# Attention with a gated MLP on one core: reciprocals read in a row, softmax sums by DMA transpose in units 0 to 115, the last head group regrouped, denser MLP tiles in the second slot

## Chip, core and metric

One core of a Trainium2 chip runs the whole kernel. The metric is the device time of one execution in microseconds; the kernel before took 1253.55 us, the median of 3 runs (1253.39 to 1253.73). One further execution was profiled: 1253.59 us, of which 1251.8 us lie between its first and its last instruction (the span).

## Reference

All tensors are bfloat16. There are 2048 tokens of width 512, 32 heads of 128 and 2048 cached keys for each head.

```
xn = layernorm(x)                                   # 2048 x 512
# A: attention
q  = xn @ wq                                        # 32 heads of 128
p  = softmax(q @ k_cache^T * 128**-0.5)             # per head 2048 x 2048
s  = concat(p @ v_cache) @ wo                       # 2048 x 512
# B: gated MLP
h  = gelu(layernorm(xn) @ w1)
hs = shift_four_column_groups_by(1, -1, 2, -2)(h) @ w2
x1 = xn + hs
g  = silu(x1 + gelu(layernorm(x1) @ w3) @ w4)
out = x + s * g
```

## The kernel before

The MLP comes first. Its last product, for token tiles 8 to 15 (128 tokens each), is held back and mixed into the first attention units as filler for TensorE: 8 tiles of 14 matmuls each (`held_part`, with VectorE's addition and ScalarE's tanh for each in `held_out`).

The attention is 128 units, `units = [(g, qt, hh)]`: 8 groups `g` of 4 heads; in each group 4 query blocks `qt` of 512 tokens; in each block the 4 heads `hh`. A unit has 8 slots `p`, and a slot `n = 8*u + p` covers 256 keys. One Python loop over `n` writes out the order of work by hand, and every instruction is pinned to that order on its engine.

Within a unit:

- `s_slot`: two matmuls of 128x512 make scores in PSUM (two buffers of 2 banks, `ps_s`), and one ScalarE exp writes `pT`.
- `pv_run`: two matmuls multiply `pT` by V into `ps_o` (two buffers), `lag` slots later. The lag is 5 in units 0 to 7, grows to 10 by unit 12, and falls back to 5 from unit `PV1` (111) on.
- `q_mm`, `q_copy`: four matmuls make the next unit's query into the PSUM tile `xa`; VectorE copies it. Sixteen units have their query made ahead, in the MLP phase (`q_ahead`: units 0 to 8, 112 to 116, 126 and 127).
- `add_first`, `add_next`, `add_last`: VectorE adds the four `pT` tiles of a unit into `acc` and folds that to 128x512 (lines 297 to 308). The rest of the row sum runs over partitions, and it has two forms.
  - `sums` (units outside `TURN`): four matmuls of one column (`ps_sum`, line 325) with `acc` as weights, then a reciprocal (line 327).
  - `turn` and `turned_sums` (units in `TURN`, which is 12 to 107): a DMA transposes `acc` into `tT` (line 333), VectorE sums along the row (line 338) and takes the reciprocal.
- Both forms write the 512 reciprocals to DRAM (`dr`) and read them back on all partitions (`bcast`: `rb`, line 346), both on SyncE's DMA queue, which works in order.
- `norm` (line 358) multiplies `ps_o` by `rb` into `oT`. A plain sum leaves on partition p the reciprocals of the queries 4p to 4p+3, a turned one those of the queries p, p+128, p+256 and p+384. So in a turned unit `rb` lies in another order than `ps_o`, and `norm` reads `rb` (float32) with a step of four elements and everything else in a row.
- `wo_mm`, `wo_post`: when the 4 heads of a block are normed, each of its 4 token tiles takes 4 matmuls with `oT` as weights into the PSUM tile `xm`, and VectorE adds the result into `sacc`. In the last group it also applies the gate and the residual (lines 411, 420, 422; for the last two query blocks 404 and 392) and the tile is stored by SyncE's queue.

Plain units do two output matmuls a slot in slots 4 and 5, turned units one a slot in slots 3 to 6. Near the end, units 125 and 126 work on two token tiles each. A block written out by hand ends unit 127 (UB): the sums and `norm` of unit 126 (UA), then `late_sums`, `late_o`, `last_wo` and the last four tiles. There, the last `norm` (unit 126) waits for the last `rb`.

```
late = 0 if u <= NU - 5 * HG else 2 if u <= NU - 5 * HG + 2 else 1
if p == (7 if u - 2 in TURN else 2 + late) and 2 <= u:
    norm_queue(u - 2)
if p == 3 + late and 1 <= u and u - 1 not in TURN:
    sums(u - 1)
```

Of the kernel before, what the change touches and what calls it, by code (L numbers as in the profile page):

```python
# [10 lines left out]
FP32 = mybir.dt.float32  # L11
BF16 = mybir.dt.bfloat16
# [5 lines left out]
def kernel(  # L18
# [16 lines left out]
    P = nc.NUM_PARTITIONS  # L35
# [3 lines left out]
    Sq, D = x2d.shape  # L39
    _, H, Sk, Dh = A_k_cache.shape  # L40
# [52 lines left out]
    psX = ent(pool("psX", 1, PSUM))  # L93
# [14 lines left out]
    def mm(out, lhsT, rhs, start, stop):  # L108
        pin(nc.tensor.matmul(out=out, lhsT=lhsT, rhs=rhs, start=start, stop=stop))  # L109
# [11 lines left out]
    LATE = (QT - 2, QT - 1)  # L121
    GY = NG - 2
    NU = len(units)
    TURN = range(3 * HG, NU - 5 * HG)
    PV0, PV1 = 2 * HG, NU - 5 * HG + 3
    NS = NU * SPU
    kTs, vBs, wqs, wos, oTs, st = {}, {}, {}, {}, {}, {}
    todo = defaultdict(list)
# [171 lines left out]
    def add_next(u, i):  # L300
        a = st[u]["acc"]
        pin(nc.vector.tensor_tensor(out=a[:], in0=a[:], in1=st[u]["pT"][i][:], op=ALU.add))  # L302

    def add_last(u):
        add_next(u, 3)
        a = st[u]["acc"]
        pin(nc.vector.tensor_tensor(out=a[:, 0:2, :], in0=a[:, 0:2, :], in1=a[:, 2:4, :], op=ALU.add))  # L307
        pin(nc.vector.tensor_tensor(out=a[:, 0, :], in0=a[:, 0, :], in1=a[:, 1, :], op=ALU.add))  # L308
# [20 lines left out]
        pin(nc.sync.dma_start(out=s["dr"][:], in_=rc[:]))  # L329

    def turn(u):
        st[u]["tT"] = pS.tile([P, 4, P], BF16, tag="tT", bufs=2, name="tT")
        pin(nc.sync.dma_start_transpose(out=st[u]["tT"][:], in_=st[u]["acc"][:, 0, :]))

    def turned_sums(u):
# [13 lines left out]
    def norm(u):  # L349
        g, qt, hh = units[u]  # L350
        s = st.pop(u)
        if hh == 0:
            oTs[(g, qt)] = pB.tile([P, HG, 512], BF16, tag="oT", bufs=2, name="oT")
        o, rb, to = s["o"][:], s["rb"][:], oTs[(g, qt)][:, hh, :]
        if u in TURN:
            o, to = (x.rearrange("k (j p) -> k j p", j=4) for x in (o, to))
            rb = rb.rearrange("k (p j) -> k j p", j=4)
        pin(nc.vector.tensor_tensor(out=to, in0=o, in1=rb, op=ALU.mult))  # L358

    wo_box = {}  # L360
# [3 lines left out]
        wos[h] = pB.tile([P, D], BF16, tag="wo", bufs=2 * HG, name="wo_h")  # L364
        pin(nc.sync.dma_start(out=wos[h][:], in_=A_wo[h * Dh:(h + 1) * Dh, :]))

    def wo_mm(g, t, hhs):
        if hhs[0] == 0:
            wo_box[0] = psX.tile([P, D], FP32, tag="xm", name="ps_wo")
        oT = oTs[(g, t // 4)]  # L370
        ts = t % 4
        for hh in hhs:
            mm(wo_box[0][:], oT[:, hh, ts * P:(ts + 1) * P], wos[g * HG + hh][:], hh == 0, hh == HG - 1)

    fin = {}

# [73 lines left out]

    def last_wo(ts, ps, hhs=(0, 1, 2), stop=False):
        for hh in hhs:
            mm(ps, oTs[(NG - 1, QT - 1)][:, hh, ts * P:(ts + 1) * P], wos[(NG - 1) * HG + hh][:],
               hh == 0, stop and hh == HG - 2)

    def last_act(ps, scale):
# [27 lines left out]
    for jc in range(DC):  # L484
        b = BASE_J[jc]
# [37 lines left out]
    made = []  # L523

    def q_ahead(u):
        q_mm(u, range(DC), ("xa", "xm")[len(made) % 2])
        q_copy(u, nc.scalar)
        made.append(u)
# [27 lines left out]
        x1(t, ps)  # L556
    for t in range(4):
        stats(xall[:, t, :], mv2, rs2, t)
    for u in range(NU - 4 * HG, NU - 3 * HG):
        q_ahead(u)  # L560
    for t in range(4, 8):
        x1(t, m2(t))
# [2 lines left out]
    m1(1536, 512)  # L565
    for t in range(8, 11):
        x1(t, m2(t))
    for u in (2 * HG, NU - 12, NU - 2, NU - 1):
        q_ahead(u)
    for t in range(4, 8):  # L570
        stats(xall[:, t, :], mv2, rs2, t)
# [39 lines left out]
    pB = left.enter_context(pool("pB", reuse_waits="tile"))  # L611
# [3 lines left out]
    pS = None  # L615
    for h in range(HG):
        load_wo(h)
    for g in range(NG - 1):
        b = (g * QT + QT - 1) * HG
# [6 lines left out]
            at((b + (-3, -3, 0, 0)[hh]) * SPU + (5, 7)[hh % 2], lambda h=h: load_w(h))  # L626
            at((b - 4 - hh // 2) * SPU + (5, 7)[hh % 2], lambda h=h: load_wo(h))

    HELD = 7
    heldps = {}  # L630

    def held_part(t, a, b, tag="xm"):
        if a == 0:
            heldps[t] = psX.tile([P, 512], FP32, tag=tag, name="ps_m")
        m4(t, heldps[t], range(a, b))

    def held_out(t, n):
        x2(t, heldps.pop(t))
        th = {}
        at(n + 2, lambda: th.update(a=gate_tanh(t)))  # L640
        at(n + 4, lambda: gate_silu(t, th["a"]))

    def held_mm(n):
        u, p = divmod(n, SPU)
        if u == 0 and p < 2:
            held_part(8, 7 * p, 7 * p + 7, "xa")
            if p == 1:
                held_out(8, n)
        elif u == 0:
            held_part(9, FC * (p - 2) // 6, FC * (p - 1) // 6)  # L650
            if p == SPU - 1:
                held_out(9, n)
        elif u < HELD:
            if p < SPU - 1:
                held_part(9 + u, 2 * p, 2 * p + 2)
            if p == SPU - 2:
                held_out(9 + u, n)

    wo_todo = deque()
    pv_at = [0]  # L660

    def pv_run(n):
        u = n // SPU
        if u < PV0:
            lag = LAG
        elif u < PV0 + LAG:
            lag = LAG + u - PV0 + 1
        elif u < PV1:
            lag = 2 * LAG
        else:  # L670
            lag = max(LAG, 2 * LAG - (u - PV1 + 1))
        while pv_at[0] <= min(n - lag, NS - 1):
            pv_slot(*divmod(pv_at[0], SPU))
            pv_at[0] += 1

    def norm_queue(u):
        norm(u)
        gg, qq, hh = units[u]
        if hh == HG - 1:
            wo_todo.extend((gg, 4 * qq + ts) for ts in range(4))  # L680
            if gg == NG - 1 and qq not in LATE:
                fin_load(4 * qq)

    UA, UB = NU - 2, NU - 1

    def wo_slot(part, n, each=2):
        gg, t = wo_todo[0]
        if part < HG // each:
            wo_mm(gg, t, tuple(range(part * each, (part + 1) * each)))
            return  # L690
        wo_todo.popleft()
        wo_post(gg, t, n)
        if gg == NG - 1 and t % 4 < 3 and t + 1 not in fin and t // 4 not in LATE:
            fin_load(t + 1)

    q_plan = defaultdict(list)
    for v in range(1, NU):
        if v not in made:
            for dc in range(DC):
                k = dc - 1 if v - 2 in TURN else dc // 2  # L700
                q_plan[(v - 1) * SPU + k].append((v, (dc,)))

    for n in range(UB * SPU):
        u, p = divmod(n, SPU)
        extra = len(wo_todo) > 3 and u < 2 * HG + 2 and pS is not None or u >= UA - 1
        s_slot(u, p)
        pv_run(n)
        for v, dcs in q_plan.get(n, ()):
            q_mm(v, dcs)
        if p == 0 and u - 2 in TURN:  # L710
            turned_sums(u - 2)
        if p == 1 and u - 2 in TURN:
            bcast(u - 2)
        if p == 0 and 1 <= u:
            add_last(u - 1)
        if p == 3 and u - 1 in TURN:
            turn(u - 1)
        if p == 0:
            twice = extra
        if twice and p < 3:  # L720
            wo_slot(p, n)
        if p == (3 if u - 1 in TURN else 2) and u + 1 not in made:
            q_copy(u + 1)
        late = 0 if u <= NU - 5 * HG else 2 if u <= NU - 5 * HG + 2 else 1
        if p == (7 if u - 2 in TURN else 2 + late) and 2 <= u:
            norm_queue(u - 2)
        if p == 3 + late and 1 <= u and u - 1 not in TURN:
            sums(u - 1)
        if p == 4 + late and 1 <= u and u - 1 not in TURN:
            bcast(u - 1)  # L730
        each, p0 = (1, 3) if u - 2 in TURN else (2, 4)
        if p0 <= p <= p0 + HG // each and wo_todo and pS is not None:
            wo_slot(p - p0, n, each=each)
        if p == 4:
            add_first(u)
        if p == 6:
            add_next(u, 2)
        held_mm(n)
        for fn in todo.pop(n, ()):
            fn()  # L740
        if n == HELD * SPU - 1:
            right.close()
            pS = right.enter_context(pool("pS", side="right", reuse_waits="tile"))

# [2 lines left out]
    n = UB * SPU  # L747
    ident2 = pS.tile([P, P], BF16, tag="ident2", name="ident2")
    pin(nc.vector.tensor_scalar(out=ident2[:], in0=ident[:], scalar1=2.0, scalar2=None, op0=ALU.mult))
    for p in range(SPU):  # L750
        s_slot(UB, p)
        pv_run(n + p)
        if p == 0:
            add_last(UA)
        if p < 2:
            wo_slot(p, n + p)
        if p == 3:
            norm(UB - 2)
            sums(UA)
            wo_slot(2, n + p)  # L760
        if p == 4:
            bcast(UA)
            add_first(UB)
        if p == 6:
            add_next(UB, 2)
# [8 lines left out]
    ps = {0: bank(psX, "xm")}  # L774
# [81 lines left out]
```

## Time and profile before

| what | value |
|---|---|
| median of 3 runs | 1253.55 us (1253.39 to 1253.73) |
| profiled execution | 1253.59 us, span 1251.8 us |
| TensorE busy | 1237.9 us, 99% of the span |
| ScalarE busy | 1101.5 us, 88% |
| VectorE busy | 1031.9 us, 82% |
| attention units start | 123.0 us |
| unit 127 starts | 1230.6 us |
| DMA queue of SyncE | 100.33 MB in 223488 packets, 37.7% of 16 engines' time |

PE is TensorE's matmul, PEld its weight load, DVE VectorE, ACT ScalarE, SPq SyncE's DMA queue. A group line of the profile names the source line, the engine, the operation, the output and inputs by the program's names, their shapes and the count; after the bar come busy us, mean ns of one, and the idle time before the group's instructions with what ended it. All matmuls go through one helper, so they share line 109 and are told apart by their tiles. A stretch row gives start and end, length, busy time with the number of instructions, granted clock and DMA.

### The profile page before, as it was taken

To read this page: it belongs to the slowest core of one execution; us is meant where nothing else is said; L and a number is where in the kernel's file an instruction comes from. 1 tells how busy PE (TensorE), PEld (TensorE's weight loads), DVE (VectorE), ACT (ScalarE), POOL (GpSimd) and SP (SyncE) were. 2 spreads that over 40 slices of the span, in tenths; PEclk is the share of its full clock that TensorE was granted. 3 is DMA by queue.
4 is the path that set the end of the run, shared out by engine and by line. 5 is a ranking of instruction groups with operands and counts; after the bars stand their busy time and mean duration, and the time that the engine had idled before them with its cause. 6 is when DMAs were issued, how large, how long until landed. Compare 5 with 4: busy or idle time off the path is not lost.

```text
span 1251.8 us, 16270 instructions
## 1 busy us (share of the span) xinstructions
PE 1237.9 (99%) x5814; PEld 597.8 (48%) x5931; DVE 1031.9 (82%) x1430; ACT 1101.5 (88%) x1117; POOL 35.5 (3%) x91
## 2 busy tenths in 40 slices
PE   9999999999999999999999999999999999999998
PEld 4444444444444444444444444444444444444443
DVE  7621567788888988888888888888888999978888
ACT  5344888999999999999999999999999999998886
POOL 5310000000000000000000000000000000000000
PEclk9999999999999999999999999999999999999999
DMA  6482112444244523453244514353244424442222
GB/s 180 112 161 54 18 26 43 87 106 81 53 89 93 118 52 64 97 110 77 68 83 106 103 39 93 80 119 68 57 100 102 103 66 86 99 92 50 68 56 59
DMA packets 224945, 103.86 MB, mean 83 GB/s; under 512 B 176928, under 2 KB 208160, under 8 KB 224864
## 3 DMA queue, kind: packets, MB, share of 16 engines
q1 hardware_dynamic: 223488, 100.33, 37.7%
q0 software_dynamic: 672, 1.84, 0.8%
q8 instruction: 46, 0.75, 0.3%
q10 hardware_dynamic: 704, 0.66, 0.2%
q14 instruction: 35, 0.29, 0.1%
HBM read 67.90 MB, written 2.36 MB: 56 GB/s over the span
## 4 chain that ended last, share of the span: by engine, by line
PE 96%; DVE 2%; issue 1%; ACT 1%; DMA 1%; POOL 0%; SPq 0%; DVEq 0%; ACTq 0%
PE ps_s L109 39%; PE ps_o L109 36%; PE ps_q L109 9%; PE ps_wo L109 9%; PE ps_m L109 2%; DVE acc L302 0%; DMA rb<-dr 0%; PE ps_sum L109 0%; PE ps_w L109 0%; DMA xin<-in_A_x_dram 0%; ACT qT L277 0%; DVE y L392 0%; DVE xall L420 0%; ACT pT L291 0%; DVE sacc L411 0%
## 5 line engine op out<-in xcount | busy, mean ns | idle before, releaser
L291 ACT ACTIVATE pT<-ps_s 128x1024 bf16<-128x1024 f32 x1024 | 1035.2, 1024 | 75.4 <-PE ps_s L109 27.8
L109 PE MATMUL ps_s<-qT,kT 128*128 128x512 bf16 x2041 | 607.6, 379 | 0.6
L109 PE MATMUL ps_o<-pT,vb 128*128 128x512 bf16 x1962 | 588.9, 379 | 0.5
L302 DVE TENSOR_TENSOR acc<-acc,pT 128x2048 bf16<-128x2048 bf16 x255 | 309.3, 1213 | 83.7 <-ACT pT L291 80.2
L109 PEld LDWEIGHTS <-kT 128*128 128x128 bf16 x2048 | 230.3, 113 | 226.6 <-issue 0.8
L109 PEld LDWEIGHTS <-vb 128*128 128x128 bf16 x2048 | 200.3, 98 | 226.4 <-issue 0.4
L109 PE MATMUL ps_wo<-wo_h,oT 128*128 128x512 bf16 x492 | 177.8, 379 | 2.1
L109 PE MATMUL ps_q<-xnT,wq_h 128*128 128x512 bf16 x481 | 172.9, 379 | 2.1
L297 DVE TENSOR_TENSOR acc<-pT 128x2048 bf16<-128x2048 bf16 x128 | 155.9, 1218 | 6.1 <-ACT pT L291 5.9
L358 DVE TENSOR_TENSOR oT<-ps_o,rb 128x512 bf16<-128x512 f32 x127 | 124.6, 981 | 15.8 <-DMA rb<-dr 15.3
L307 DVE TENSOR_TENSOR acc<-acc 128x1024 bf16<-128x1024 bf16 x127 | 87.9, 692 | 4.3
L275 DVE CAST qT<-ps_q 128x512 bf16<-128x512 f32 x112 | 76.5, 683 | 0.3 <-PE ps_q L109 0.3
L109 PEld LDWEIGHTS <-oT 128*128 128x128 bf16 x508 | 48.5, 98 | 56.1 <-DVE oT L358 0.7
L109 PEld LDWEIGHTS <-wq_h 128*128 128x128 bf16 x484 | 47.2, 98 | 56.1 <-issue 0.2
L411 DVE TENSOR_TENSOR sacc<-ps_wo,sacc 128x512 f32<-128x512 f32 x96 | 66.3, 691 | 3.2 <-PE ps_wo L109 2.7
L338 DVE TENSOR_REDUCE sm<-tT 128x4 f32<-128x512 bf16 x96 | 65.5, 682 | 0.5 <-DMA tT<-acc 0.4
L308 DVE TENSOR_TENSOR acc<-acc 128x512 bf16<-128x512 bf16 x127 | 54.0, 425 | 4.3
L242 ACT ACTIVATE h2T<-ps_s 128x1024 bf16<-128x1024 f32 x28 | 28.7, 1025 | 24.0 <-PE ps_s L109 24.0
L109 PE MATMUL ps_s<-xn2T,w_sb 128*128 128x512 bf16 x219 | 48.6, 379 | 0.3
L109 PEld LDWEIGHTS <-w_sb 128*128 128x128 bf16 x336 | 30.3, 98 | 32.1
L109 PEld LDWEIGHTS <-h2T 128*128 128x128 bf16 x224 | 21.5, 98 | 25.0 <-issue 0.2
L109 PE MATMUL ps_m<-w_sb,h2T 128*128 128x512 bf16 x106 | 31.0, 379 | 0.5
(75 smaller groups left out, 334.7 us busy)
## 6 DMA issues: line engine op xcount, KB each, us to landing
rb<-dr SPq DMA_DIRECT2D x127, 256.0 KB, 3.9
vb<-in_A_v_cache_dram SPq DMA_DIRECT2D x64, 256.0 KB, 3.1
wq_h<-in_A_wq_dram SPq DMA_DIRECT2D x32, 128.0 KB, 3.1
wo_h<-in_A_wo_dram SPq DMA_DIRECT2D x32, 128.0 KB, 3.1
w_sb<-in_B_w_dram SPq DMA_DIRECT2D x8, 256.0 KB, 4.9
kT<-in_A_k_cache_dram SPq DMA_TRANSPOSE x128, 3.0
xl<-in_A_x_dram SPq DMA_DIRECT2D x16, 128.0 KB, 3.6
dr<-rc SPq DMA_DIRECT2D x127, 2.0 KB, 1.4
```

Of the source, the lines that this page charges most:

```text
L109: pin(nc.tensor.matmul(out=out, lhsT=lhsT, rhs=rhs, start=start, stop=stop))
L242: pin(nc.scalar.activation(out=h2[c, f][:], in_=ps[:], func=ACT.Gelu_apprx_tanh))
L275: pin(nc.vector.tensor_copy(out=qT[:], in_=st[u].pop("psq")[:]))
L291: pin(nc.scalar.activation(out=s["pT"][-1][:, jj:jj + 2, :], in_=sps[:], func=ACT.Exp, scale=SCALE))
L297: pin(nc.vector.tensor_tensor(out=s["acc"][:], in0=s["pT"][0][:], in1=s["pT"][1][:], op=ALU.add))
L302: pin(nc.vector.tensor_tensor(out=a[:], in0=a[:], in1=st[u]["pT"][i][:], op=ALU.add))
L307: pin(nc.vector.tensor_tensor(out=a[:, 0:2, :], in0=a[:, 0:2, :], in1=a[:, 2:4, :], op=ALU.add))
L308: pin(nc.vector.tensor_tensor(out=a[:, 0, :], in0=a[:, 0, :], in1=a[:, 1, :], op=ALU.add))
L338: pin(nc.vector.tensor_reduce(out=sm[:], in_=s["tT"][:], axis=mybir.AxisListType.X, op=ALU.add))
L358: pin(nc.vector.tensor_tensor(out=to, in0=o, in1=rb, op=ALU.mult))
L411: pin(nc.vector.tensor_tensor(out=sa, in0=ps[:], in1=sa, op=ALU.add))
```

## The change

1. `TURN` is now units 0 to 115, so 116 units sum by DMA transpose instead of 96. Plain sums remain in units 116 to 126, and 127 keeps its own. `tT` moves to the pool that is open from the first unit on.
2. In turned units `norm` reads `rb` and writes `oT` in a row, and reads `ps_o` with a step of 128 float32 elements (512 B). `oT` then holds the queries in another order, and the output matmuls read their weights from it with a step of four elements (`o_cols`).
3. `PV1` moves from 111 to 119, and the lag is 10 from the first unit on.
4. The held MLP matmuls run 4 and 10 in slots 0 and 1, then 3 a slot up to slot 9, then 2 a slot in slots 0 to 4 of a unit and 1 in slots 5 to 7.
5. In plain units the output matmuls go one a slot in slots 4 to 7, and their `wo_post` comes at slot 0 of the next unit; `norm` is at slot 4, `sums` at 5. Two token tiles are now worked on in units 121 and 126 instead of 125 and 126. In unit 127 one more `wo_post` stands at slot 0, and the other stands ahead of `norm` and `sums`.
6. The query matmuls go one a slot everywhere. Fifteen units have theirs made ahead: 0 to 8, 120 to 124 and 127.
7. In turned units `norm` comes after `wo_post` in slot 7.

```diff
-    TURN = range(3 * HG, NU - 5 * HG)
-    PV0, PV1 = 2 * HG, NU - 5 * HG + 3
+    TURN = range(NU - 3 * HG)
+    PV1 = NU - 3 * HG + 3
...
-        st[u]["tT"] = pS.tile([P, 4, P], BF16, tag="tT", bufs=2, name="tT")
+        st[u]["tT"] = pB.tile([P, 4, P], BF16, tag="tT", bufs=2, name="tT")
...
         if u in TURN:
-            o, to = (x.rearrange("k (j p) -> k j p", j=4) for x in (o, to))
-            rb = rb.rearrange("k (p j) -> k j p", j=4)
+            o = o.rearrange("k (j p) -> k p j", j=4)
+            rb, to = (x.rearrange("k (p j) -> k p j", j=4) for x in (rb, to))
         pin(nc.vector.tensor_tensor(out=to, in0=o, in1=rb, op=ALU.mult))
...
+    def o_cols(g, qt, hh, ts):
+        o = oTs[(g, qt)][:, hh, :]
+        if (g * QT + qt) * HG + hh in TURN:
+            return o.rearrange("k (p j) -> k j p", j=4)[:, ts, :]
+        return o[:, ts * P:(ts + 1) * P]
...
-    for u in range(NU - 4 * HG, NU - 3 * HG):
+    for u in range(NU - 2 * HG, NU - HG):
         q_ahead(u)
...
-    for u in (2 * HG, NU - 12, NU - 2, NU - 1):
+    for u in (2 * HG, NU - 1, NU - HG):
         q_ahead(u)
...
+    held = deque((t, fc) for t in range(8, NT) for fc in range(FC))
...
     def held_mm(n):
...
+        for _ in range((4, 10)[n] if n < 2 else 3 if n < 2 * LAG else 2 if n % SPU < 5 else 1):
+            if not held:
+                return
+            t, fc = held.popleft()
+            if fc == 0:
+                heldps[t] = psX.tile([P, 512], FP32, tag=("xa", "xm")[t % 2], name="ps_m")
+            m4(t, heldps[t], (fc,))
+            if fc == FC - 1:
+                held_out(t, n)
...
     def pv_run(n):
         u = n // SPU
-        if u < PV0:
-            lag = LAG
-        elif u < PV0 + LAG:
-            lag = LAG + u - PV0 + 1
-        elif u < PV1:
+        if u < PV1:
             lag = 2 * LAG
...
-        extra = len(wo_todo) > 3 and u < 2 * HG + 2 and pS is not None or u >= UA - 1
+        extra = len(wo_todo) > 3 and u < 2 * HG + 2 and pS is not None
+        if p == 0 and wo_box:
+            wo_slot(4, n, each=1)
...
-        late = 0 if u <= NU - 5 * HG else 2 if u <= NU - 5 * HG + 2 else 1
-        if p == (7 if u - 2 in TURN else 2 + late) and 2 <= u:
+        if u - 2 < TURN.start:
+            norm_p, sum_p, wo_p, each = 2, 3, 4, 2
+        elif u - 2 in TURN:
+            norm_p, sum_p, wo_p, each = 7, 5, 3, 1
+        else:
+            norm_p, sum_p, wo_p, each = 4, 5, 4, 1
+        if p == norm_p and 2 <= u and not u - 2 in TURN:
             norm_queue(u - 2)
-        if p == 3 + late and 1 <= u and u - 1 not in TURN:
+        if p == sum_p and 1 <= u and u - 1 not in TURN:
             sums(u - 1)
...
-        each, p0 = (1, 3) if u - 2 in TURN else (2, 4)
-        if p0 <= p <= p0 + HG // each and wo_todo and pS is not None:
-            wo_slot(p - p0, n, each=each)
+        if u in (NU - 7, UA) and p in (1, 2, 3):
+            wo_slot(p - 1, n)
+        if wo_p <= p <= wo_p + HG // each and wo_todo and pS is not None:
+            wo_slot(p - wo_p, n, each=each)
+        if p == norm_p and u - 2 in TURN:
+            norm_queue(u - 2)
...
         if p == 0:
+            wo_slot(4, n, each=1)
             add_last(UA)
-        if p < 2:
-            wo_slot(p, n + p)
+        if p in (1, 2, 3):
+            wo_slot(p - 1, n + p)
         if p == 3:
             norm(UB - 2)
             sums(UA)
-            wo_slot(2, n + p)
```

More of the change, by code (lines that the diff above doesn't have):

```diff
@@ L365, in load_wo, with wo_mm @@
         pin(nc.sync.dma_start(out=wos[h][:], in_=A_wo[h * Dh:(h + 1) * Dh, :]))
-    def wo_mm(g, t, hhs):
+    def o_cols(g, qt, hh, ts):
[3 more added lines that the diff above has]
+        return o[:, ts * P:(ts + 1) * P]
+    def wo_mm(g, t, hhs, tag="xm"):
         if hhs[0] == 0:
-            wo_box[0] = psX.tile([P, D], FP32, tag="xm", name="ps_wo")
-        oT = oTs[(g, t // 4)]
+            wo_box[0] = psX.tile([P, D], FP32, tag=tag, name="ps_wo")
         ts = t % 4
         for hh in hhs:
-            mm(wo_box[0][:], oT[:, hh, ts * P:(ts + 1) * P], wos[g * HG + hh][:], hh == 0, hh == HG - 1)
+            mm(wo_box[0][:], o_cols(g, t // 4, hh, ts), wos[g * HG + hh][:], hh == 0, hh == HG - 1)
     fin = {}
@@ L452, in last_wo @@
         for hh in hhs:
-            mm(ps, oTs[(NG - 1, QT - 1)][:, hh, ts * P:(ts + 1) * P], wos[(NG - 1) * HG + hh][:],
+            mm(ps, o_cols(NG - 1, QT - 1, hh, ts), wos[(NG - 1) * HG + hh][:],
                hh == 0, stop and hh == HG - 2)
@@ L627 @@
             at((b - 4 - hh // 2) * SPU + (5, 7)[hh % 2], lambda h=h: load_wo(h))
-    HELD = 7
     heldps = {}
[L632 to L635, printed above, removed]
+    held = deque((t, fc) for t in range(8, NT) for fc in range(FC))
     def held_out(t, n):
@@ L643, in held_mm @@
     def held_mm(n):
[L644 to L657, printed above, removed]
+        for _ in range((4, 10)[n] if n < 2 else 3 if n < 2 * LAG else 2 if n % SPU < 5 else 1):
[7 more added lines that the diff above has]
+                held_out(t, n)
     wo_todo = deque()
@@ L684, with wo_slot @@
     UA, UB = NU - 2, NU - 1
-    def wo_slot(part, n, each=2):
+    def wo_slot(part, n, each=2, **kw):
         gg, t = wo_todo[0]
         if part < HG // each:
-            wo_mm(gg, t, tuple(range(part * each, (part + 1) * each)))
+            wo_mm(gg, t, tuple(range(part * each, (part + 1) * each)), **kw)
             return
@@ L699 @@
             for dc in range(DC):
-                k = dc - 1 if v - 2 in TURN else dc // 2
+                k = dc - 1 if v - 2 >= TURN.start else dc // 2
                 q_plan[(v - 1) * SPU + k].append((v, (dc,)))
@@ L720 @@
         if twice and p < 3:
-            wo_slot(p, n)
-        if p == (3 if u - 1 in TURN else 2) and u + 1 not in made:
+            wo_slot(p, n, tag="xa")
+        if p == (3 if u - 1 >= TURN.start else 2) and u + 1 not in made:
             q_copy(u + 1)
-        late = 0 if u <= NU - 5 * HG else 2 if u <= NU - 5 * HG + 2 else 1
-        if p == (7 if u - 2 in TURN else 2 + late) and 2 <= u:
+        if u - 2 < TURN.start:
[5 more added lines that the diff above has]
+        if p == norm_p and 2 <= u and not u - 2 in TURN:
             norm_queue(u - 2)
-        if p == 3 + late and 1 <= u and u - 1 not in TURN:
+        if p == sum_p and 1 <= u and u - 1 not in TURN:
             sums(u - 1)
-        if p == 4 + late and 1 <= u and u - 1 not in TURN:
+        if p == sum_p + 1 and 1 <= u and u - 1 not in TURN:
             bcast(u - 1)
-        each, p0 = (1, 3) if u - 2 in TURN else (2, 4)
-        if p0 <= p <= p0 + HG // each and wo_todo and pS is not None:
-            wo_slot(p - p0, n, each=each)
+        if u in (NU - 7, UA) and p in (1, 2, 3):
[4 more added lines that the diff above has]
+            norm_queue(u - 2)
         if p == 4:
@@ L740 @@
             fn()
-        if n == HELD * SPU - 1:
+        if pS is None and not held:
             right.close()
```

## Prediction

> **What bounds the kernel now.** I read first the page's busy shares, clock and chain.
>
> ```profile
> PE 1237.9 (99%) x5814; PEld 597.8 (48%) x5931; DVE 1031.9 (82%) x1430; ACT 1101.5 (88%) x1117; POOL 35.5 (3%) x91
> PEclk9999999999999999999999999999999999999999
> PE 96%; DVE 2%; issue 1%; ACT 1%; DMA 1%; POOL 0%; SPq 0%; DVEq 0%; ACTq 0%
> ```
>
> TensorE is busy for 99% of the span at the full granted clock and is 96% of the chain. A busy PE may still be slower than its best, so the next view is TensorE's weight loads by stretch (one load for each matmul, so the count in brackets counts matmuls).
>
> ```profile
> 133.83:203.00 69.17, 33.59 (x345) 1.00 0.13 24
> 203.00:245.46 42.46, 20.55 (x211) 1.00 0.36 76
> 642.59:677.12 34.53, 16.60 (x160) 1.00 0.43 88
> 1074.04:1142.40 68.36, 33.27 (x342) 1.00 0.42 82
> 1142.40:1221.83 79.43, 38.66 (x397) 1.00 0.20 57
> ```
>
> The third row is four turned units: 34.53 us / 160 = 0.2158 us for each 128x512 matmul, and all turned units keep this pace. It is the yardstick. The others are plain units, whose counts hold four loads of `acc` for each sum. Row 1 (units 1 to 7): 28 such loads and one that straddles the edge leave 316 matmuls, 68.20 us at the yardstick; 0.97 us are over. Row 2 (units 8 to 12): 191 matmuls, 41.22 us, 1.24 us over. Row 4 (units 109 to 116): 310 matmuls, 66.91 us, 1.45 us over. Row 5 (117 to 125): 360 matmuls, 77.70 us, 1.73 us over. So PE loses time only where plain sums stand. The timeline shows how:
>
> ```profile
> 206.97 0.42 PEld L109 LDWEIGHTS <-acc 128*128 128x128 bf16 x4
> 207.21 0.27 PE L109 MATMUL ps_sum<-ones_t,acc 128*128 128x1 bf16 x4
> 207.31 0.15 PEld L109 LDWEIGHTS <-kT 128*128 128x128 bf16 x2
> ```
>
> From the first `ps_sum` at 207.21 to the next score matmul at 207.34 are 0.13 us. The rest of a group's loss (0.14 to 0.25 us a unit) is uneven slots: four matmuls are 0.86 us, while ScalarE's exps follow each other at about 0.9 us (starts at 1235.02, 1235.95, 1236.88), so short slots end with TensorE waiting for an exp.
>
> **Sums removed.** 20 plain sums go (units 0 to 11 and 108 to 115, run one unit later). Their units become turned ones, with one query or output matmul in each slot, the form that holds 0.2158. Gain: 0.97 + 1.24 + 1.45 = 3.66 us. If the uneven slots stayed, it would be 20 x 0.13 = 2.6 us.
>
> **What they cost elsewhere.** Each adds a transposing DMA (landing 3.7 us median) and a 0.68 us reduce on VectorE. The reduce and the strided norm make a VectorE busy time of 30.28 us in 34.53 in the steady units, so it is hidden there, and the queue order in slots 0, 1 and 3 is that of the 96 units that already do it. I take nothing.
>
> **Norm.** The groups, and VectorE's busy time by stretch (steady, then units 96 to 107):
>
> ```profile
> L358 DVE TENSOR_TENSOR oT<-ps_o,rb 128x512 bf16<-128x512 f32 x127 | 124.6, 981 | 15.8 <-DMA rb<-dr 15.3
> L109 PEld LDWEIGHTS <-kT 128*128 128x128 bf16 x2048 | 230.3, 113 | 226.6 <-issue 0.8
> L109 PEld LDWEIGHTS <-oT 128*128 128x128 bf16 x508 | 48.5, 98 | 56.1 <-DVE oT L358 0.7
> 642.59:677.12 34.53, 30.28 (x40) 1.00 0.43 88
> 962.03:1065.63 103.60, 99.08 (x134) 1.00 0.42 90
> ```
>
> The mean of 981 ns mixes 683 ns for plain units and 1077 ns where `rb` is read with a step of 16 B. The changed norm steps 512 B through PSUM, which no row shows: it costs 0.68 us if PSUM does not mind, 1.08 if it minds as SBUF does, more if it is worse. I take 1.08, the nearest row. Either way VectorE fits below 8.63 us a unit, so PE's time is the same and the term is 0.
>
> [...]
>
> Output weights are now read with a step of four bfloat16, as `kT` is: 113 instead of 98 ns, under a matmul of 216. Score matmuls behind such loads keep the yardstick, so this is 0; if the cover went, 464 x 0.015 = 7 us.
>
> **Queries made ahead.** One fewer: four matmuls (0.86 us) leave the MLP phase, where PE runs without gaps at that place (42.8 to 46.2 us), and enter the loop. Sum 0.
>
> **Start.** The first two slots hold 18 matmuls in both versions, so slot 2 meets the first exp at 126.9 us as now. After that five matmuls a slot (1.08 us) stand against an exp of 0.9 to 1.02 and two tanh of 0.63 in slots 3 and 8. I take 0.05 us of waiting, bounds 0 to 0.5 (the present 0.04 in unit 0 could also go).
>
> **Units 117 to 126.** Ten sums remain. Row 5 holds a stall that I can name: in unit 125 two 1.8 us posts stand ahead of the norm, which ends at 1219.40; the first PV matmul needs the PSUM buffer that this norm reads, and starts at 1219.46, 0.24 us late. The change takes the second tile out of unit 125: -0.24. But now a post stands at slot 0 in every unit and pushes the norm back, while PV at lag 5 starts in slot 5. By VectorE's starts in unit 125 and 126 (post 1.87 us, add 1.26, folds 0.73 and 0.34, query copy 0.60, norm 0.68, from 0.15 on) the norm ends 5.6 us into units 124 and 125; in 126, with two posts of 1.33 and no copy, 5.8. PV wants it after 26 or 27 matmuls, 5.6 to 5.8. I take three waits of 0.07, +0.2 us, bounds 0 to 0.9 (three times what unit 125 shows).
>
> **Unit 127.** Timeline of VectorE, SyncE's queue and the weight loads:
>
> ```profile
> 1231.96 1.23 DVE L302 TENSOR_TENSOR acc<-acc,pT 128x2048 bf16<-128x2048 bf16 x1
> 1235.49 0.18 DVE L327 RECIPROCAL rc<-ps_sum 128x4 f32<-128x4 f32 x1 [0.52 <-PE ps_sum L109]
> 1235.70 0.32 SPq L329 DMA_DIRECT2D dr<-rc  x1
> 1237.01 0.34 SPq L393 DMA_DIRECT2D out_dram<-y  x1
> 1237.44 0.38 SPq L346 DMA_DIRECT2D rb<-dr  x1
> 1241.46 0.69 DVE L358 TENSOR_TENSOR oT<-ps_o,rb 128x512 bf16<-128x512 f32 x1 [0.49 <-DMA rb<-dr]
> 1242.20 0.10 PEld L109 LDWEIGHTS <-oT 128*128 128x128 bf16 x1 [0.67 <-DVE oT L358]
> ```
>
> The last `rb` lands, VectorE has waited 0.49 us for it, TensorE 0.67 us for the norm, and all that follows hangs on it. The change puts two posts (`tm`, `y`: 1.4 us each) ahead of the reciprocal. Its new start: slot 0's scores begin at 1230.87 and the first `tm` 0.2 later; from unit 126's starts, `tm` to `y` is 0.72 us, `y` to the add 0.61, add to fold 1.26, to the second fold 0.73, to `tm` 0.34, to `y` 0.72, to the norm 0.61, to the reciprocal 0.73: 5.72 us, so 1236.79, 1.30 later than now. `y`'s store, which today holds `rb` back from 1237.10 (where `dr` landed) to 1237.44, has gone ahead: -0.34. Sum: +0.96, I take +1.0. `dr` lands 1.4 us after issue, at times 2.1 to 2.8 with `rb` then quicker; bounds +0.5 to +1.8.
>
> **Sum**, against the profiled 1253.59 us (span 1251.8 and 1.8 around it): -3.66 + 0.05 - 0.24 + 0.2 + 1.0 = -2.65, so 1250.94. The median before is 0.04 lower: 1250.9 us. By 0.2% (2.5 us, about what a measurement of this kernel can tell from no change) the line to "faster" is at 1251.04, so the forecast lies almost on it.
>
> **Rivals.**
>
> 1. *The end costs nothing*: `rb` comes as early as now, and the new waits of units 124 to 126 stay away. Then 1250.9 - 1.0 - 0.2 = 1249.7. For it: spread slots may win some of row 5's 1.49 us. Against: VectorE's order is fixed, and 0.49 us of waiting for `rb` leaves no cover. Chance 0.15.
> 2. *The end costs its upper bounds*: norm before PV waits 0.24 in each of three units and `rb` is 1.8 late: 1250.9 + 0.5 + 0.8 = 1252.2. Unit 125 shows the first; the variation of `dr` the second. Chance 0.17.
> 3. *The sums were cover*: in the former plain units another wait (an exp, `tT`) takes the place of the removed groups, and only the bare 2.6 us or less is won: 1252.0, or 1253.5 if half of that goes. Against: no turned unit in the third row's form leaves 0.2158. Chance 0.07.
> 4. *Slower*: the PSUM step makes the norm cost far more. VectorE idles (103.60 - 99.08) / 12 = 0.38 us a unit in units 96 to 107, so from 1.08 + 0.38 = 1.45 us on it sets the pace there. At 2.15, twice the strided row, 12 units lose 0.70 each, 8.4 us, less some 1.7 of slack before PV wants the buffer: 1250.9 + 6.7 = 1257.6. Chance 0.06. [...]
>
> **How the numbers follow.** The forecast, 1250.2 to 1251.8, has 0.55; a little over half of it is past the line to faster. Faster: 0.33 + 0.15 = 0.48. Slower, past 1256.06: 0.06. Same: 0.46. The range runs from 1249.5, just under rival 1, to 1252.8, past rival 2 and the first part of 3; rival 4, the worst of 3 and the tails of the others are left out.
>
> **What the profile after would show.** Units 1 to 11 and 109 to 116 at 0.2158 a matmul (if not, rival 3); 44 `ps_sum` matmuls from `acc` with `ones_t` instead of 124; norm rows near 0.68 or 1.08 (above 1.45: rival 4); the last reciprocal about 5.9 us after unit 127's first scores instead of 4.6, with VectorE's last wait for `rb` at about 1.5 us instead of 0.49. If that reciprocal is no later, rival 1 holds; if weight loads stall on `oT` in units 118 to 126, rival 2. A total over 1253.5 would break the accounting as a whole.

## The result and the profile after

The changed kernel takes 1251.53 us, the median of 22 runs (1251.21 to 1252.71), against 1253.54 us for the kernel before in the same series (22 runs, 1253.22 to 1254.31). The ratio is 0.9984, with an interval of 0.9978 to 0.9990: 0.16% faster, 0.6 us above the forecast of 1250.9 and short of the line to "faster" at 0.2%. The profiled execution took 1251.28 us with a span of 1249.3 us. First the page's busy time of TensorE and its chain:

```profile
PE 1240.9 (99%) x5851; PEld 603.2 (48%) x5851; DVE 1007.9 (81%) x1451; ACT 1111.0 (89%) x1116; POOL 35.4 (3%) x91
PE 95%; DVE 2%; DMA 2%; ACT 1%; issue 0%; POOL 0%; DVEq 0%
```

TensorE still sets the time. The chain has 2% of DMA where it had 1%, which is the first hint at what was overlooked. Next, weight loads by stretch, for units 1 to 7, 8 to 12, four steady units, 109 to 116, and 117 to 125 (start and end, length, busy time with the count, granted clock, DMA share, GB/s):

```profile
133.05:199.74 66.69, 32.10 (x310) 1.00 0.21 42
199.74:242.91 43.17, 21.07 (x201) 1.00 0.42 87
640.31:674.84 34.53, 16.88 (x160) 1.00 0.46 85
1071.98:1141.29 69.31, 33.77 (x321) 1.00 0.52 92
1141.29:1218.85 77.56, 38.27 (x390) 1.00 0.22 59
```

Counts 1, 2, 4 and 5 hold one load that straddles an edge. Rows 1 and 2 are 309 and 200 matmuls: 66.69 and 43.17 us at 0.2158 us each, so nothing is left over. Row 4 is 320 matmuls, 69.06 us, and 0.25 us are over; they lie in one place, which is met below. Row 5 holds 9 sums of 4 loads and 353 matmuls: 76.18 us, 1.38 us over, 0.15 for each sum.

Put side by side by the first load of each unit's keys, the two profiled executions differ as follows (the forecast's terms put in the same places):

| stretch | before | after | difference | forecast |
|---|---|---|---|---|
| up to unit 0 | 123.00 | 122.65 | -0.35 | -0.86 |
| units 0 to 12 | 122.46 | 120.26 | -2.20 | -2.16 |
| units 13 to 107 | 820.17 | 820.44 | +0.27 | 0 |
| units 108 to 126 | 164.99 | 164.35 | -0.64 | -0.63 |
| unit 127 to the end | 21.20 | 21.63 | +0.43 | +1.00 |
| outside the span | 1.77 | 1.95 | +0.18 | 0 |
| sum | 1253.59 | 1251.28 | -2.31 | -2.65 |

The norm and the output weights, by groups:

```profile
L358 DVE TENSOR_TENSOR oT<-ps_o,rb 128x512 bf16<-128x512 f32 x127 | 86.7, 683 | 11.7 <-DMA rb<-dr 11.6
L109 PEld LDWEIGHTS <-oT 128*128 128x128 bf16 x508 | 56.8, 112 | 59.7 <-DVE oT L358 1.3
```

The step of 512 B through PSUM costs nothing here: 683 ns, what the plain units' norm took before. VectorE's busy time in the four steady units falls with it:

```profile
640.31:674.84 34.53, 29.00 (x41) 1.00 0.46 85
```

It was 30.28 us, with one instruction fewer at the edges. The output's weight load went from 98 to 112 ns, under the matmuls. The end of unit 127, by the timeline of VectorE and SyncE's queue:

```profile
1233.70 0.17 DVE L327 RECIPROCAL rc<-ps_sum 128x4 f32<-128x4 f32 x1
1233.90 0.33 SPq L329 DMA_DIRECT2D dr<-rc  x1
1235.31 0.33 SPq L346 DMA_DIRECT2D rb<-dr  x1
1239.25 0.69 DVE L358 TENSOR_TENSOR oT<-ps_o,rb 128x512 bf16<-128x512 f32 x1 [1.41 <-DMA rb<-dr]
```

The reciprocal comes 5.75 us after the unit's first scores (4.62 before), `rb` is issued as soon as `dr` has landed, and VectorE waits 1.41 us for it where it waited 0.49.

Three waits in this trace were not in the forecast's sum. One is in the MLP phase, where TensorE's timeline has

```profile
47.67 1.67 PE L109 MATMUL ps_o<-w_sb,hT 128*128 128x512 bf16 x7 [0.25 <-DVE xall L225]
```

The four query matmuls that left this place had covered VectorE's statistics (up to 47.0 us); without them the next product waits. The other two are in units 31 (8.91 us instead of 8.63) and 111 (8.87). By the timeline of VectorE and the weight loads, in unit 111:

```profile
1091.55 0.69 DVE L358 TENSOR_TENSOR oT<-ps_o,rb 128x512 bf16<-128x512 f32 x1 [1.08 <-DMA rb<-dr]
...
1092.30 0.10 PEld L109 LDWEIGHTS <-vb 128*128 128x128 bf16 x1 [0.36 <-issue]
```

VectorE waits 1.08 us for `rb`, so the norm ends at 1092.24, and only then may PV write into the PSUM buffer that this norm read. The loads follow at 0.459 us instead of 0.216: 0.24 lost.

**Where the late `rb` comes from.** Units 15, 31, 47 and so on up to 111 are the last of a head group. In the units before them (14, 30, 46 and on) SyncE's queue loads V of the next group's second head. That load waits for the last PV matmuls of an earlier head (in unit 110 it waited 4.2 us, until 2.35 us into the unit), so the reciprocals of these units stand behind it and come late. SyncE's timeline in unit 46, before:

```profile
532.71 0.38 SPq L150 DMA_DIRECT2D vb<-in_A_v_cache_dram  x1
533.15 1.14 SPq L140 DMA_TRANSPOSE kT<-in_A_k_cache_dram  x1
534.38 0.53 SPq L342 DMA_DIRECT2D dr<-rc  x1
536.32 0.32 SPq L346 DMA_DIRECT2D rb<-dr  x1
```

and after:

```profile
530.43 0.38 SPq L150 DMA_DIRECT2D vb<-in_A_v_cache_dram  x1
530.86 1.14 SPq L140 DMA_TRANSPOSE kT<-in_A_k_cache_dram  x1
532.10 0.53 SPq L342 DMA_DIRECT2D dr<-rc  x1
535.23 0.32 SPq L346 DMA_DIRECT2D rb<-dr  x1
```

The issue is 4.02 us into the unit in both, behind the same loads, yet `dr` (2 KB) needs 3.1 instead of 1.9 us. Over all seven such units it is 3.1 to 3.5 against 1.6 to 2.6, from the issue of `dr` to that of `rb`. The DMA view of after, from 1084.5 to 1086.5 us in unit 110, names a guest:

```profile
q8 instruction: 1, 0.02, 4.3%
```

One packet of the instruction queue takes 4.3% of 16 engines for 2 us, 1.4 us of one engine. The profile's page has 46 of these packets, 0.75 MB: 16 KB each, for 11702 matmuls and weight loads, so one for each 254 (the first kernel of experiment 3, with 872 more of them, has 49). A head group of 16 turned units is 16 x 40 x 2 = 1280 instructions, and both traces have five packets in each from unit 14 to unit 109: the packet falls at the same point of each group. Before, it fell 6.2 to 6.8 us ahead of these seven units, in most 6.7. The change takes 12 sums of 8 instructions and 4 query matmuls with their loads out of what precedes unit 13: 104 instructions, 52 x 0.2158 = 11.2 us, so the packet comes 4.5 us into them, and the trace has 4.4 to 5.1, onto the V load, the K load and `dr`. That the packets are TensorE's code is read from this count and from where they fall. The theory to test: TensorE's code fetch holds an engine that `dr` needs.

### The profile page after: what moved, and what is told of

Read it like the earlier page. It is cut to its first block, busy times and chain, and to the rows that moved or that the text cites. A ratio compares the mean times of both kernels' runs of the same rounds, so it can differ in the third digit from the quotient of the medians.

```text
span 1249.3 us, 16259 instructions
## 1 busy us (share of the span) xinstructions
PE 1240.9 (99%) x5851; PEld 603.2 (48%) x5851; DVE 1007.9 (81%) x1451; ACT 1111.0 (89%) x1116; POOL 35.4 (3%) x91
## 4 chain that ended last, share of the span: by engine, by line
PE 95%; DVE 2%; DMA 2%; ACT 1%; issue 0%; POOL 0%; DVEq 0%
PE ps_s L109 39%; PE ps_o L109 37%; PE ps_wo L109 8%; PE ps_q L109 8%; PE ps_m L109 2%; DMA rb<-dr 1%; DMA dr<-rc 1%; DVE acc L302 0%; DVE oT L358 0%; DVE bn L180 0%; DVE y L397 0%; PE ps_w L109 0%; DMA xin<-in_A_x_dram 0%; ACT qT L277 0%; DVE acc L307 0%; ACT pT L291 0%
## 5 line engine op out<-in xcount | busy, mean ns | idle before, releaser
L109 PE MATMUL ps_o<-pT,vb 128*128 128x512 bf16 x2048 | 607.5, 379 | 0.2
L109 PE MATMUL ps_wo<-wo_h,oT 128*128 128x512 bf16 x496 | 186.7, 379 | 0.0
L109 PE MATMUL ps_q<-xnT,wq_h 128*128 128x512 bf16 x488 | 180.1, 379 | 0.0
L358 DVE TENSOR_TENSOR oT<-ps_o,rb 128x512 bf16<-128x512 f32 x127 | 86.7, 683 | 11.7 <-DMA rb<-dr 11.6
L109 PEld LDWEIGHTS <-oT 128*128 128x128 bf16 x508 | 56.8, 112 | 59.7 <-DVE oT L358 1.3
L338 DVE TENSOR_REDUCE sm<-tT 128x4 f32<-128x512 bf16 x116 | 78.6, 677 | 0.7 <-DMA tT<-acc 0.5
```

The costliest lines, as they stand in the source:

```text
L338: pin(nc.vector.tensor_reduce(out=sm[:], in_=s["tT"][:], axis=mybir.AxisListType.X, op=ALU.add))
```

## The experiments

**1. The norm's order undone in the changed kernel, and alone in the kernel before.** In the first, `rb` is again read with a step, `oT` is written as before and the output weights are read in a row (the diff shows the norm alone); the second is the kernel before with the new norm and `o_cols` alone.

```diff
-            o = o.rearrange("k (j p) -> k p j", j=4)
-            rb, to = (x.rearrange("k (p j) -> k p j", j=4) for x in (rb, to))
+            o, to = (x.rearrange("k (j p) -> k j p", j=4) for x in (o, to))
+            rb = rb.rearrange("k (p j) -> k j p", j=4)
```

> The changed kernel with one part undone: the norm of turned units reads rb with a step of four again and ps_o in a row, and the output weights are read in a row. TensorE theory (the gain is 20 plain sums and the uneven slots around them, and VectorE has room): norm back at 1.08 us, steady units still 8.63 us, total 1251.5 within 0.5; the only places that can react are the units at a group border, where the norm already comes late (units 31 and 111 lost 0.28 and 0.24 us in the profile), so at most seven times 0.4 = 2.8 us more. VectorE rival (the gain is the 0.39 us that each of 116 norms lost): most of the 2 us goes, about 1253.5, with waits spread over ordinary units.

> The kernel before with this one part added: norm of the turned units 12 to 107 reads rb and writes oT in a row, ps_o with a step of 512 B, output weights with a step of four. TensorE theory: norm 0.68 instead of 1.08 us, VectorE's busy time 37 us less, units still 8.63 us, total 1253.5 within 0.4. VectorE rival: 1251.5 to 1252.5.

The first took 1255.96 us against 1254.18 for before on the same chip, ratio 1.0014 (1.0005 to 1.0022); the second 1254.05, ratio 0.9999 (0.9991 to 1.0008). So the cheaper norm is worth nothing alone, and yet the rest of the change without it is slower than before. The first kernel's ordinary units still take 8.63 us; nearly all its loss is in units 15, 31, 47, 63, 79, 95 and 111 (0.29 to 0.92 us each, 3.9 in all). Its timeline in units 110 and 111, of SyncE, VectorE and the weight loads:

```profile
1087.24 0.53 SPq L342 DMA_DIRECT2D dr<-rc  x1
1090.98 0.32 SPq L346 DMA_DIRECT2D rb<-dr  x1
1094.47 1.05 DVE L358 TENSOR_TENSOR oT<-ps_o,rb 128x512 bf16<-128x512 f32 x1 [1.39 <-DMA rb<-dr]
1095.58 0.10 PEld L109 LDWEIGHTS <-vb 128*128 128x128 bf16 x1 [1.04 <-issue]
```

`dr` takes 3.7 us, and a norm of 1.05 us on top makes PV wait. It is the wait of unit 111 above, in all seven places. Neither a general VectorE limit nor a general TensorE gain explains that; it is tied to a place.

**2. The code fetch moved away, and moved in.** 25 matmuls of one column with their weight loads, of no use, go ahead of the attention loop of the slow kernel of experiment 1, and 75 into the kernel before at the same place (the tile they write is read by nobody). They shift the fetches; the time that they take themselves lies ahead of the attention's start.

```diff
+    shift = psX.tile([P, 4], FP32, tag="xa", name="ps_shift")
+    for _ in range(25):
+        mm(shift[:, 0:1], ident[:], ones_t[:], True, True)
```

> The kernel of a1 (changed kernel, norm reading rb with a step) with 25 pairs of a weight load and a one-column matmul put in front of the attention loop; they shift TensorE's instruction count, and with it the moment at which its next 16 KB of code is fetched over a DMA engine. Code-fetch theory: the waits of 0.3 to 0.9 us in units 15, 31, 47, 63, 79, 95 and 111 (3.9 us in all) come from a code fetch that falls 4.4 to 5.3 us into units 14, 30, 46, 62, 78, 94 and 110, onto the DMA engine that the V load, the kT load and dr of that moment use; 25 pairs move it 5.4 us earlier within the unit pattern, so the waits go and the pairs cost 25 x 0.032 = 0.8 us: 3.1 us below a1. VectorE rival (the longer norm itself makes the waits): they stay, and the time is a1 plus 0.8.

> The kernel before with 75 such pairs in front of the attention loop. Code-fetch theory: they move the fetch from 6.7 us before units 30, 46, 62, 78, 94 to about 4.6 us into them; dr lands there 3 to 3.5 us after its issue instead of 1.6 to 2.6, and the units after lose 0.3 to 0.9 us each, 2 to 4 us in all, on top of 75 x 0.032 = 2.4 us: 1258.5 to 1260.5 against 1254.2. VectorE rival or any theory in which the border waits come from the change's own order of work: no waits at the borders, 1256.6.

With 25 the slow kernel runs at 1251.86 us against 1253.99, ratio 0.9983 (0.9974 to 0.9993), 3.9 us less than without them beside its chip's before. The fetches now fall between 1.2 us ahead of the start of the seven units and 0.4 us behind it, no unit from 14 to 111 is longer than 8.64 us, and the same `dr` by SyncE's timeline takes 1.9 us:

```profile
1085.15 0.53 SPq L342 DMA_DIRECT2D dr<-rc  x1
1087.01 0.32 SPq L346 DMA_DIRECT2D rb<-dr  x1
```

With 75 the kernel before goes to 1259.18 us, ratio 1.0046 (1.0031 to 1.0061): its attention starts 2.07 us later, its fetches fall 5.2 to 5.8 us into the seven units, and units 15, 31, 47, 63, 66, 79 and 95 lose 0.30 to 0.79, 3.8 us in all. Work that does nothing made one kernel 4 us faster, and another 3 us slower beyond the time that this work takes. The theory holds in both directions. Two places differ: unit 66 is no border (there an `rb` landed 5.8 us after its issue, with a fetch in that time), and unit 110 has plain sums in this kernel, with its `dr` elsewhere, so unit 111 lost nothing. With the fetches away, the kernel with the strided norm is as fast as the changed one (0.9983 and 0.9984), so by itself the cheaper norm is worth nothing here either.

**3. What the removed sums were worth.** Two runs: four one-column matmuls with `acc` as weights in each turned unit from 8 on (109 groups, the result is not used; the diff shows the call alone), and the changed kernel with the old uneven slots (two query or output matmuls a slot).

```diff
+        if p == 5 and 8 <= u and u - 1 in TURN:
+            idle_sums(u - 1)
```

```diff
-                k = dc - 1 if v - 2 >= TURN.start else dc // 2
+                k = dc // 2
...
-        if p == (3 if u - 1 >= TURN.start else 2) and u + 1 not in made:
+        if p == 2 and u + 1 not in made:
...
-            norm_p, sum_p, wo_p, each = 7, 5, 3, 1
+            norm_p, sum_p, wo_p, each = 7, 5, 4, 2
```

> The changed kernel with four more one-column matmuls (acc as weights, result unused) in slot 5 of units 8 to 116, 109 groups: the bare cost of a plain sum on TensorE, with slots left as they are. TensorE theory: 0.13 us each, 14.2 us more, total 1265.7, every steady unit 8.76 instead of 8.63 us. If a group hides behind other work (an exp that ends later anyway): less than 4 us. If each also makes the next score matmul wait as in the plain units before (0.15 to 0.25): 16 to 27 us more.

> The changed kernel with the query matmuls two a slot in slots 0 and 1 and the output matmuls two a slot in slots 4 and 5, as plain units had them, sums still by DMA transpose: slots of 6 and of 4 matmuls instead of 5. TensorE theory with ScalarE's exp as the other side: the four-matmul slots (0.86 us) fall behind the exp (0.9) and each unit loses about 0.1 us as units 8 to 11 did beside their sum: 8 to 13 us more, 1260 to 1264, with score matmuls waiting at the short slots. Rival (the even slots are worth nothing, the sums alone cost): 1251.5 within 1.

The idle groups: 1266.1 us against 1254.18, ratio 1.0098 (1.0084 to 1.0112), with 8.77 us a unit, 0.14 more. With before's ratio of the changed kernel (0.9984) the same chip would give it 1252.2, so a group costs 13.9 / 109 = 0.13 us. The uneven slots: 1255.76 us, ratio 1.0012 (1.0003 to 1.0021). A unit takes 8.67 instead of 8.63 us: 0.04 us, less than half of what was expected (unit 47 lost another 0.73 behind a late `dr`). Waits of its ScalarE, from 123 to 1140 us (total, times, longest):

```profile
ACT pT L291 <- PE ps_s L109: 90.5, 350, 0.6
```

It was 6.8 us, 26 times, in the changed kernel. ScalarE waits much more, but TensorE hardly notices. The lag of 10 slots is the likely reason; no run varies it.

**4. Fewer warm-up matmuls.** The changed kernel's first 11 matmuls, whose result is not used, are cut to 5, with 20 of 64 columns behind them: another way to move the fetches.

```diff
-    warm_mm(11)
+    warm_mm(5)
+    for _ in range(20):
+        mm(wps[:, 0:64], warm[:, 0:P], warm[:, 0:64], True, True)
```

> The changed kernel with the last 6 of the 11 warm-up matmuls of 512 columns replaced by 20 of 64 columns: 14 pairs more at about the same length, so code fetches fall 3.0 us earlier in the unit pattern, 1.5 us into the border units, ahead of the V load at 2.35. Code-fetch theory: dr at the borders lands in 1.6 to 2.6 us instead of 3.1 to 3.5, units 31 and 111 lose nothing, span 0.5 us shorter (if the start is not later). Rival: the waits stay as in the changed kernel's profile.

1252.73 us in a single run, with a span of 1250.8. The fetches fall 1.8 to 2.3 us into the seven units and none of their successors waits, as the theory says, but the attention starts 1.73 us late (0.24 of it because the first input came later). Busy time from 6 to 12 us (PE, PEld, DVE, ACT, POOL, then the granted clock), changed kernel and this one:

```profile
6.00:12.00 6.00, 5.50 (x84) 4.69 (x83) 5.83 (x16) 4.50 (x12) 4.40 (x11) 1.00 1.10 290
```

```profile
6.00:12.00 6.00, 5.39 (x62) 5.07 (x63) 5.83 (x17) 2.90 (x7) 4.44 (x10) 0.72 1.10 286
```

The granted clock fell to 0.72, and 62 matmuls were done in place of 84. The cut warm-up was also shorter, against what was expected: it ran for 3.38 us instead of 4.74, and TensorE then stood idle for 1.54 us until the first normed tile was there. So the run does not tell whether the narrow matmuls or this gap lost the clock. The edit moved more than the fetches, so only the loop speaks for the theory.

**5. The reciprocal of the end ahead of the last post again.** The changed kernel, but unit 126 does its second tile two matmuls a slot and posts it in slot 7, so that unit 127 has no post at slot 0, and the last post stands behind the reciprocal and the broadcast of `rb` instead of ahead of them.

```diff
-        if wo_p <= p <= wo_p + HG // each and wo_todo and pS is not None:
+        if u == UA:
+            if p in (4, 5):
+                wo_slot(p - 4, n)
+        elif wo_p <= p <= wo_p + HG // each and wo_todo and pS is not None:
             wo_slot(p - wo_p, n, each=each)
...
+        if p == 7 and u == UA:
+            wo_slot(2, n)
...
         if p == 0:
-            wo_slot(4, n, each=1)
             add_last(UA)
-        if p in (1, 2, 3):
+        if p in (1, 2):
             wo_slot(p - 1, n + p)
...
         if p == 4:
             bcast(UA)
+            wo_slot(2, n + p)
             add_first(UB)
```

> The changed kernel with the end reordered: unit 126 works its second tile two matmuls a slot in slots 4 and 5 and posts it in slot 7, so nothing is posted in slot 0 of unit 127, and the last post comes behind the reciprocal and behind the broadcast of unit 126. Theory of the end (the last rb sets it): the reciprocal starts 4.7 us into unit 127 instead of 5.75, rb lands about 10.2 instead of 11.2, VectorE waits for it 0 to 0.3 us instead of 1.41, and the end comes 0.9 to 1.1 us earlier, less up to 0.2 for uneven slots in unit 126. Rival (the final matmuls hang on something else, the last exp or TensorE's own count): 0.3 us or less.

1251.57 us against 1253.99, ratio 0.9981 (0.9971 to 0.9990). From unit 127 to the end it takes 20.70 instead of 21.63 us, 0.93 less, and the last norm comes without waiting for `rb`. The median does not show it: 0.9981 is no clear step from the changed kernel's 0.9984, as the intervals overlap. The profiled execution lost 1.65 us in units 15, 31, 47 and 63, where the changed kernel's lost 0.5 in units 31 and 111: how often the fetch delays `dr` enough differs from one execution to the next.

**6. The version that these point to, and the price of a turned unit.** On one chip: the changed kernel; the same with experiment 5's tail and 13 one-column pairs in the MLP phase, where TensorE waits for VectorE at 47.67 us anyway; and the changed kernel with plain sums again in units 7 to 11 and 108 to 115, their slots left even (of this one the diff shows the first line alone).

```diff
+    shift = psX.tile([P, 4], FP32, tag="xm", name="ps_shift")
+    for _ in range(13):
+        mm(shift[:, 0:1], ident[:], ones_t[:], True, True)
```

```diff
-    TURN = range(NU - 3 * HG)
+    TURN = set(range(NU - 5 * HG)) - set(range(7, 12))
```

> The changed kernel once more, as the reference on the same chip for the two kernels beside it. About 1251.5 us; its code fetches fall 4.4 to 5.1 us into the units before a new head group, and units 14 to 111 lose 0.5 to 1.7 us to PV matmuls that wait for the norm of such a unit.

> The changed kernel with the end of unit 127 in the old order, and 13 one-column matmul pairs put into the MLP phase at a place where TensorE waits 0.34 us for VectorE anyway. Theory (code fetch meets the chain of the reciprocals): the pairs move every later fetch about 2.8 us earlier, to some 1.7 to 2.3 us into the units before a new head group, no PV matmul waits in the units behind them, so 0.5 to 1.7 us are won there; the end wins 0.9; the pairs cost 0.1 or nothing. Together 1249 to 1250.2 against about 1251.5 for the changed kernel. Rival (the waits come from the order of the norm on VectorE and not from the fetch): they stay, and only the end wins: 1250.6.

> The changed kernel with plain sums again in units 7 to 11 and 108 to 115 (13 groups), everything else as changed. Theory: 13 x 0.13 = 1.7 us are given back, in units 8 to 12 and 109 to 116; the 20 added weight loads and 20 matmuls ahead of unit 14 move the code fetches 4.3 us earlier, near the start of the units before a new head group, so the waits of 0.5 to 1.7 us behind those go: 0 to 1.2 us above the changed kernel. Rival (a turned unit is worth its whole 0.18 us a unit, and the fetch is of no account): 13 x 0.18 = 2.4 us above it.

| kernel | median, us | ratio to before (1254.39) | interval |
|---|---|---|---|
| changed | 1252.90 | 0.9988 | 0.9980 to 0.9997 |
| tail and 13 pairs | 1250.12 | 0.9965 | 0.9951 to 0.9979 |
| 13 plain sums back | 1254.05 | 0.9999 | 0.9990 to 1.0007 |

The second beats both kernels; it is 2.8 us below the changed one, a little more than was expected. In the profiles its fetches fall 1.8 to 2.4 us into the seven units, and units 15 and 47 lose 0.18 us where the changed kernel lost 1.0 (units 31, 47, 79, 111). The attention starts 0.28 us later, but so did the first input (VectorE's first statistics at 4.05 against 3.78 us); from there to the attention both kernels take 119.2 us, so the pairs cost nothing. The end won 0.64: `rb` took 4.7 us here. These make 1.2 us of 1.3 in the profiled spans. The profiled execution was this kernel's slowest run (1251.13), so of the 2.8 us between the medians about half is not located. In the third kernel units 8 to 12, 109 to 114 and 116 take 8.77 us, 0.13 to 0.14 more each, fetches fall at 0.5 us before to 0.7 us after the start of the seven units and no wait follows there; unit 115 lost 0.81 us beyond its sum to a late load of `kT`, once, behind a `dr` of 4.1 us with no fetch near it, which no theory had. 1.15 us above the changed kernel is inside its expectation, and far from the rival's 2.4.

**All traces together.** The thirteen traces hold 91 units of the kind of 14, 30 and on to 110. In the 37 where a code packet starts within 2 us after `dr` is issued, `dr` takes 3.1 to 4.2 us, with one exception of 2.6. In the other 54 it takes 1.6 to 2.7. So at this place the packet's moment decides whether `dr` is late. That it does so by holding an engine that `dr` needs is the likely reading, but not shown: the traces do not say on which of the 16 engines a packet ran. At other places `dr` can be late without a packet (3.0 us in unit 67 of the changed kernel).

## Why the prediction came out as it did

The likeliest case happened, and the total landed in its own range, above the line to "faster", where the chances had stood at 0.48 for faster and 0.46 for the same. That it landed so close is partly luck: the late `rb` (+0.5) and the lost cover in the MLP phase (+0.34) were in no term, and the end and units 117 to 126 came out about 0.8 us better than forecast.

- **Sums removed (-3.66).** Right: -2.20 us in units 0 to 12 and no excess left in units 1 to 12; units 109 to 116 keep only the 0.24 us of unit 111. The 0.13 us for a group is confirmed (experiments 3 and 6). The rest, 1.06 us, was put down to uneven slots; it was 0.01 us a unit in units 1 to 7, 0.12 in units 8 to 12 and 0.05 in units 109 to 116. Uneven slots alone cost 0.04 in a turned unit with the long lag, so in units 8 to 12 they are at most a third of it by this measure, and what made up the remainder there is not shown. It went with the regrouping as a whole. Rival 3, the sums as cover, is out.
- **What they cost elsewhere (0).** Right for ordinary units, wrong at the seven group borders: +0.51 us (units 31 and 111) in this execution, 1.0 and 1.65 in others. The step that failed is the zero for this term, with its reason that "the queue order in slots 0, 1 and 3 is that of the 96 units that already do it". The order was the same; the time at which TensorE's code arrives was not, since a change in the number of matmuls moves all later fetches (104 instructions fewer took them from 6.7 us ahead of these units to 4.4 to 5.1 us into them). The trace of before showed the packets, and the prediction did not look at them.
- **Norm (1.08 us taken).** It measured 0.68. Rival 4 fell with it; its 2.15 us was the author's doubling of the strided row, and no run shows it. The 1.08 was the price of the 16 B step in SBUF (1077 ns), put on a step through PSUM that no row had shown; the 683 ns with the step of 512 B show no penalty. That the term is 0 at either price was wrong, too: with the fetch at the border, the kernel with a 1.05 us norm lost 3.9 us there, the one with 0.68 between 0.5 and 1.65. The prediction weighed a norm against VectorE's mean time a unit, not against a late `rb`.
- **Queries ahead (0).** -0.86 and +0.86 are there, but the wait at 47.67 us took 0.34 of the first back (the loads' steps over 0.216 us at this place were 0.297, 0.221 and 0.296, and are 0.631 and 0.298). "PE runs without gaps" was true because of these four matmuls. Another 0.17 us of the start is a later first input (VectorE's first statistics at 3.48 instead of 3.31 us).
- **Units 117 to 126 (-0.24 and +0.2).** Unit 125's stall is gone. PV waited for the norm in 124, 125 and 126 for 0.04, 0.04 and 0.10 us: 0.17. In units 117 to 125 the excess still fell from 1.73 to 1.38 us, 0.1 more than unit 125's stall, though two of these waits are in it; rival 1 had named "spread slots" for such a gain, and it came without that rival's early `rb`. It offsets unit 111 in the table.
- **Unit 127 (+1.0).** The mechanism was right, its size was not: +0.43. The reciprocal is 1.13 us later (1.30 forecast), the way from it to the norm 0.42 shorter (0.34 forecast), so the norm is 0.71 later; and from there to the end it takes 10.05 instead of 10.34 us, which was in no step and was not followed further. Experiment 5 confirms the place: with the reciprocal ahead of the last post 0.93 comes back.

## What to carry to other kernels

When TensorE sets the time and the number of its instructions changes, look where its code packets fall in the new trace, against the short DMAs that others wait for: the phase alone moved two of these kernels by 3 to 4 us, more than the change that was tried. A fixed phase can be set by a few one-column matmuls at a place where TensorE waits anyway (13 pairs in experiment 6, at no cost: 119.2 us up to the attention with and without). And when work is taken away from a place without gaps, ask which wait that work had covered (0.34 us here).

## What the runs showed of the hardware

- A code packet of 16 KB took 0.88 to 1.43 us in nine of ten cases (599 packets in thirteen traces). Where it fell beside a 256 KB load and a 2 KB write, the write took 3.1 to 4.2 us (once 2.6) instead of 1.6 to 2.7. The other units of the changed kernel's steady loop that hold a packet kept their 8.63 us. So a packet by itself cost TensorE nothing there; where a short transfer on the path shared its moment, the unit behind lost up to 0.92 us (experiment 1).
- In the norm VectorE read float32 from PSUM with a step of 512 B at the price of a read in a row (683 ns for 128x512), while a step of 16 B in SBUF took 1077 ns.
- With a warm-up of five 512-column and twenty 64-column matmuls (3.38 us, then 1.54 us idle) the granted clock was 0.72 from 6 to 12 us; with eleven of 512 columns (4.74 us) it was 1.00. Which of width, length and gap did it is open.
